# Float64 weights to float32: one VectorE shift-and-or in place of a VectorE shift and a GpSimd integer sum, and all weight remainders on VectorE

## The chip, the core and the metric

One core of a Trainium2 chip runs the whole program. Its engines are TensorE (PE; PEld is its weight load), VectorE (DVE), ScalarE (ACT), GpSimd (POOL) and SyncE (SP), whose queue issues the transfers here. The metric is the device time of one execution in microseconds (us), lower is better.

## The reference

Four batches of an attention with a linear memory beside it, then two feed-forward blocks over the 2304 tokens:

```python
a = softmax(causal(q @ k.T / 8)); local = a @ v               # B=4, H=8, S=576, D=64
mem = (phi(q) @ M_prev) / (phi(q) . z_prev + 1e-6)
x = sigmoid(beta) * mem + (1 - sigmoid(beta)) * local          # tokens x 512
x = ((x @ w1) * (x @ w2)) @ w3 @ w_out                         # 512 -> 1024 -> 512
out = (sigmoid(x @ w_gate) * (x @ w_val)) @ moe2_w_out         # 512 -> 1536 -> 512
```

The feed-forward weights arrive as float64, 8 bytes a number. The kernel has to make float32 of them on the chip.

## The kernel before, in words

**Work and stages.** The batches run one after another, and batch b's feed-forward part (`ffn`) is woven with batch b+1's attention (`attention`). In the profile the feed-forward products carry the names of what they make: `wps` (a product of w3 and w_out, made once, by `prep`), `ab` (x with w1 and w2), `xw` (times that product), `gv` (gate and value), `ot` (the output). Each weight is used as a float32r head plus a float32r remainder, so a product takes three matmuls. PE's order is written out by hand; the other engines' orders come from a scheduler that goes by priority, and that follows the order in which the program emits its steps.

**The weights' way.** All 76 float64 pieces (128 x 512 numbers, 512 KB each) are converted in batch 0, inside the first 370 us. A piece goes like this:

- SP loads it to `r` (line 279; three buffers).
- `conv_step`, step 0: ACT makes `cy` from the high words (L307) and `cr` from the low words (L308). `cy` are the bits of the float32 result, shifted right by three places; `cr` is the low word's top three bits, rounded to an integer from 0 to 8. Two buffers each. The next load is emitted here, too.
- step 1: DVE shifts `cy` left by three into `wraw` (L316; three buffers of two pieces each).
- step 2: POOL adds `cr` to `wraw` as integers (L320). A second piece of a unit that is needed again whole is then written to DRAM as `kf` (L322).
- `split_step` calls `split_rows`: ACT copies `wraw` to a float32r head (L549), and DVE or POOL takes the remainder (L551), into `wslot` (a ring of five) or, for w_out, `wo`. `SHARE_W` says which engine: 0.2 of the pieces on POOL in the start, 0.5 in batch 0's feed-forward. What later batches read again is written to DRAM as `k` (L419).

`pump`, called after every second group of matmuls, emits at most one `conv_step` and one `split_step`; `prep` emits one or the other per yield while the first four `wo` pieces are missing.

**What else is on these engines around there.** POOL scales the attention's probabilities `p` (L870) and takes two products of the memory path, `me` and `mphi` (L782, L791). DVE takes the score reductions (L844), the products `hraw` and `hgraw` (L623, L688), and the remainders of activations, `h` and `hg` (L551 too). ACT takes the exponentials (L116), the sigmoid of the gate, `gsb` (L116), and copies out of PSUM. After the conversion the `wraw` buffers hold `wagain`, weights read back from `kf`, of which `make_step` makes sums (`wmade`) for later batches.

Of the kernel before, what the change touches and what calls it, by code (L numbers as in the profile page):

```python
# [10 lines left out]
U32 = mybir.dt.uint32  # L11
# [3 lines left out]
AF = mybir.ActivationFunctionType  # L15
ALU = mybir.AluOpType
# [19 lines left out]
P0 = 8  # L36
NPREP = 4

SHARE_W = (0.2, 0.5, 0.0, 0.0)
SHARE_H = (0.0, 0.0, 0.3, 0.4)  # L40
SHARE_X = (0.0, 0.4, 0.5, 0.5)
SHARE_N = (1.0, 0.5, 0.5, 0.5)
# [5 lines left out]
EXPO = 0x7F800000  # L48
TOP = 2.0**13
MOST = 2.0**45  # L50

FRAC = 0.96
FA = (1.0, 1.0)
# [6 lines left out]
def tile_attention_memory_ffn(  # L60
# [17 lines left out]
    nc = tc.nc  # L78
# [58 lines left out]
    def power(out, back, sums):  # L137
# [4 lines left out]
        nc.vector.tensor_scalar(a, sums.bitcast(I32), EXPO, EXPO, ALU.bitwise_and, ALU.bitwise_xor)  # L142
        nc.vector.tensor_scalar(out, a.bitcast(F32), TOP, MOST, ALU.mult, ALU.min)
        nc.vector.tensor_scalar(b, out.bitcast(I32), EXPO, EXPO, ALU.bitwise_and, ALU.bitwise_xor)
# [80 lines left out]
    ws = {"conv": 0, "step": 0, "split": 0, "ring": 0, "freed": 0, "use": 0, "again": 0, "mstep": 0, "pumps": 0, "late": 0, "scaled": 0, "wo": 0, "pass": 0, "wready": False}  # L225
    tmp = {}
# [47 lines left out]
    def load64(n):  # L274
        if n < len(conv_slots):
            s = conv_slots[n]
            t = fp.tile([128, 512], I64, tag="r64", name=f"r64_{s}", bufs=R64)
            src = units[s // 2][0][s % 2]
            d = nc.sync.dma_start(out=t, in_=src.rearrange("p a c -> p (a c)"))
            raw64[s] = t  # L280
            last["dma"] = d

    def whole(u, hf):
        return raws[u][:, 4 * hf : 4 * hf + 4, :].rearrange("p a c -> p (a c)").bitcast(I32)

    def conv_step():
        s = ws["conv"]
        u, hf = divmod(s, 2)
        if u >= NU or (ws["step"] == 0 and ws["split"] < 2 * (u - 2)):
            return False  # L290
        src = units[u][0]
        if not isinstance(src, list):
            if not ws["wready"]:
                return False
            raws[u] = fp.tile([128, 8, 128], F32, tag="wraw", name=f"wraw{u}", bufs=3)
            last["dma"] = nc.sync.dma_start(out=raws[u], in_=src)
            ws["conv"] += 2
            return True
        if ws["step"] == 0:
            w = raw64.pop(s).bitcast(I32).rearrange("p (c two) -> p c two", two=2)  # L300
            y = fp.tile([128, 512], F32, tag="cy", name=f"cy{s}", bufs=2)
            r = fp.tile([128, 512], I32, tag="cr", name=f"cr{s}", bufs=2)
            hi = w[:, :, 1].bitcast(F32)

            nc.scalar.activation(out=y, in_=hi, func=AF.Prelu, scale=2.0**-112, alpha=2.0**32)  # L307
            nc.scalar.activation(out=r, in_=w[:, :, 0].bitcast(U32), func=AF.Copy, scale=2.0**-29)  # L308
            load64(conv_rank[s] + R64)
            tmp["y"], tmp["r"] = y.bitcast(I32), r  # L310
            ws["step"] = 1
        elif ws["step"] == 1:
            if hf == 0:
                raws[u] = fp.tile([128, 8, 128], F32, tag="wraw", name=f"wraw{u}", bufs=3)
            y, z = tmp["y"], whole(u, hf)
            nc.vector.tensor_scalar(z, y, 3, None, ALU.logical_shift_left)  # L316
            ws["step"] = 2
        else:
            z = whole(u, hf)
            nc.gpsimd.tensor_tensor(z, z, tmp["r"], ALU.add)  # L320
            if hf == 1 and u in kept:
                nc.sync.dma_start(out=kept[u], in_=raws[u])  # L322
            ws["step"] = 0
            ws["conv"] += 1
        return True
# [12 lines left out]
    def make_step():  # L338
# [21 lines left out]
        src = src[:, 0::3] if m == 0 else src[:, 1:3]  # L360
        split_rows(t.rearrange("p x (a b) c -> p x a (b c)", b=2), src, SHARE_W)
        nc.sync.dma_start(out=summed[makes[k]][m], in_=t.bitcast(F32))
# [32 lines left out]
    def split_step():  # L395
# [7 lines left out]
        if not units[u][1]:  # L403
# [4 lines left out]
            wot[m] = t  # L408
            split_rows(t[:, :, :DM].rearrange("p x (a c) -> p x a c", c=128), r, SHARE_W)
            ws["wo"] += 1  # L410
        else:
# [3 lines left out]
            w = fp.tile([128, 2, 4, 128], F32R, tag="wslot", name=f"wslot{n}", bufs=RING)  # L415
            split_rows(w, r, SHARE_W)
            if s in stored:
# [8 lines left out]
    def pump():  # L426
        late_scale()
        late_load()
        conv_step()
        split_step()  # L430
        ws["pumps"] += 1
        if phase["n"] == 2 and ws["pumps"] % 2 == 0:
            make_step()

    def need(store, s):
        while s not in store:
            moved = split_step()
            moved = conv_step() or moved
            ws["pumps"] += 1
            late_scale()  # L440
            late_load()
            assert moved
        return store[s]
# [104 lines left out]
    def split_rows(dst, src, share=None):  # L548
        nc.scalar.copy(dst[:, 0], src)  # L549
        eng = lower(share) if share else nc.vector  # L550
        eng.tensor_sub(dst[:, 1], src, dst[:, 0].bitcast(F32))  # L551

    def prep(g):
        p, f0 = divmod(2 * g, F1)
        for m in range(4 * p, 4 * p + 4):
            while m not in wot:
                if not split_step():
                    conv_step()
                yield WAIT
# [622 lines left out]
```

## Time and profile before

| what | before |
|---|---|
| median of 3 runs | 1068.26 us (1065.63 to 1071.70) |
| the profiled execution's own time | 1070.48 us |
| its span (first to last instruction) | 1068.70 us |
| PE busy | 1029.2 us, 96% |
| DVE busy | 610.9 us, 57% |
| ACT busy | 559.5 us, 52% |
| POOL busy | 401.7 us, 38% |

Busy times are sums over the span, so an average over stages that have different limits. PE's busy time includes the tail of matmuls whose ends are modelled, so a stage with PE at 96% may still have room. The stages in the profile's time: the start (attention of batch 0 and the first half of `wps`) up to 129 us, `ab` to 240, `xw` to 272, `gv` to 352, `ot` to 402, and then batch 1. The clock of PE is full in most slices; it reads 0.87 and 0.74 of full in 40 to 80 us.

### The profile page before, as it was taken

The numbers are of one execution on the slowest core, as the hardware profiler recorded it, in microseconds if no ns is written. First come the engines' busy times: TensorE is split into PE (matmuls) and PEld (weight loads), VectorE is DVE, ScalarE is ACT, GpSimd is POOL, SyncE is SP. The second block draws the span as 40 slices with busy tenths as digits, with TensorE's granted clock in tenths as the row PEclk, the third lists the DMA queues.
The fourth block names the chain that finished last, engine by engine and source line by source line (L and its number), as shares of the span: only waits on it lengthen the run. The fifth ranks groups of instructions, "written<-read, shape, count | busy, mean of one in ns | idle before, by whom it ended". The sixth has DMA issues, their size and how long they took to land.

```text
span 1068.7 us, 20275 instructions
## 1 busy us (share of the span) xinstructions
PE 1029.2 (96%) x7408; PEld 892.7 (84%) x7408; DVE 610.9 (57%) x1457; ACT 559.5 (52%) x1195; POOL 401.7 (38%) x352
## 2 busy tenths in 40 slices
PE   7899999999999998999999998999999999999998
PEld 3455687888999898898998886777999898899998
DVE  6765678756567657995755438754666321226630
ACT  6877687657767735564533444564544332224420
POOL 5967576436567702332233102322334200003320
PEclk9889999999999999999999998999999999999999
DMA  8664799958999589994688646522599543248981
GB/s 264 199 204 135 245 331 342 330 178 301 302 348 333 181 309 407 337 333 142 226 305 292 195 146 232 177 73 73 177 331 324 187 139 132 82 155 308 324 286 54
DMA packets 92667, 252.13 MB, mean 236 GB/s; under 512 B 11544, under 2 KB 30104, under 8 KB 92568
## 3 DMA queue, kind: packets, MB, share of 16 engines
q1 hardware_dynamic: 92568, 250.84, 68.4%
q8 instruction: 59, 0.97, 0.4%
q14 instruction: 40, 0.33, 0.1%
HBM read 186.31 MB, written 64.49 MB: 235 GB/s over the span
## 4 chain that ended last, share of the span: by engine, by line
PE 66%; DMA 6%; DVE 4%; issue 2%; ACT 2%; POOL 2%; SPq 1%; DVEq 0%; POOLq 0%; ACTq 0%
PE gvp L476 16%; PE ab L465 16%; PE ot L465 10%; PE xw L465 9%; PE gv L465 5%; PE s L839 3%; PE t L900 3%; PE o L968 2%; DMA wagain<-kf 2%; DMA wslot<-s 2%; PE o L953 1%; DMA k<-wslot 1%; PE o L961 1%; DMA wraw<-kf 1%; POOL wraw L320 1%
## 5 line engine op out<-in xcount | busy, mean ns | idle before, releaser
L465 PE MATMUL ab<-x,wslot 128*128 128x288 f32 (+1 forms) x1536 | 221.4, 297 | 0.4 <-DMA wslot<-k 0.4
L476 PE MATMUL gvp<-x,wslot 128*128 128x288 f32 x1512 | 204.5, 296 | 4.8 <-DMA wslot<-s 3.1
L476 PEld LDWEIGHTS gvp<-x,wslot 128*128 128x128 f32 x1512 | 202.0, 188 | 7.0 <-DVE hgraw L545 4.8
L870 POOL TENSOR_SCALAR p<-p,sm,omg 116x116 f32<-116x116 f32 (+4 forms) x100 | 88.3, 886 | 220.3 <-DVE sm L868 151.3
L465 PE MATMUL ot<-hg,wslot 128*128 128x288 f32 x1152 | 163.7, 298 | 1.3 <-DVE hg L551 1.3
L465 PEld LDWEIGHTS ot<-hg,wslot 128*128 128x128 f32 x1152 | 154.4, 188 | 7.4 <-issue 5.1
L116 ACT ACTIVATE p<-p,sm 116x116 f32<-116x116 f32 (+4 forms) x160 | 93.2, 583 | 68.8 <-DVE sm L844 65.8
L320 POOL TENSOR_TENSOR wraw<-wraw,cr 128x512 int32<-128x512 int32 x76 | 110.1, 1463 | 29.0 <-DVE wraw L316 26.8
L465 PE MATMUL xw<-h,wslot 128*128 128x288 f32 x768 | 111.9, 299 | 1.2 <-DVE h L551 0.9
L465 PEld LDWEIGHTS ab<-x,wslot 128*128 128x128 f32 x768 | 105.5, 190 | 8.1 <-issue 5.6
L465 PEld LDWEIGHTS xw<-h,wslot 128*128 128x128 f32 x768 | 103.3, 188 | 4.9 <-issue 2.4
L844 DVE CUSTOM_DVE_ANT_0 p<-s,msk 116x116 f32<-116x116 f32 (+4 forms) x160 | 68.3, 453 | 63.3 <-PE s L839 62.7
L465 PEld LDWEIGHTS <-wslot 128*128 128x128 f16 x768 | 74.0, 99 | 22.1 <-issue 3.1
L900 PE MATMUL t<-idf,p 116*116 116x116 f32 x480 | 70.5, 275 | 11.6 <-DVE sm L867 4.7
L465 PE MATMUL gv<-x,wslot 128*128 128x288 f32 x576 | 78.3, 296 | 2.0 <-DVE hgraw L688 1.4
L465 PEld LDWEIGHTS gv<-x,wslot 128*128 128x128 f32 x576 | 76.6, 188 | 3.6 <-DVE hgraw L688 2.5
L900 PEld LDWEIGHTS t<-idf,p 116*116 116x116 f32 x480 | 54.7, 140 | 27.6 <-ACT p L116 7.2
L526 POOL TENSOR_TENSOR u4gv<-u2gv,s5gv 128x288 f32<-128x288 f32 x36 | 29.3, 813 | 116.4 <-ACT s5gv L524 74.0
L551 POOL TENSOR_TENSOR wslot<-wraw,wslot 128x512 fp32r<-128x512 f32 x36 | 47.8, 1327 | 52.6 <-ACT wslot L549 49.0
L623 DVE TENSOR_TENSOR hraw<-ab,asb 128x288 f32<-128x288 f32 x64 | 29.1, 454 | 62.8 <-PE ab L465 60.3
L307 ACT ACTIVATE cy<-r 128x512 f32<-128x512 f32 x76 | 50.4, 672 | 24.1 <-DVE wraw L316 12.0
L308 ACT ACTIVATE cr<-r 128x512 int32<-128x512 uint32 x76 | 50.9, 671 | 12.1 <-POOL wraw L320 11.4
(127 smaller groups left out, 1547.0 us busy)
## 6 DMA issues: line engine op xcount, KB each, us to landing
wslot<-k SPq DMA_DIRECT2D x112, 512.0 KB, 4.7
wslot<-s SPq DMA_DIRECT2D x72, 512.0 KB, 4.9
k<-wslot SPq DMA_DIRECT2D x48, 512.0 KB, 4.7
r<-in_gv_dram SPq DMA_DIRECT2D x24, 512.0 KB, 5.4
s<-wmade SPq DMA_DIRECT2D x24, 512.0 KB, 5.6
kf<-wraw SPq DMA_DIRECT2D x20, 512.0 KB, 5.3
qk<-in_qk_dram SPq DMA_DIRECT2D x32, 290.0 KB, 4.3
wslot<-k SPq DMA_DIRECT2D x36, 256.0 KB, 4.6
```

What stands on the lines that cost most here:

```text
L116: ins = nc.scalar.activation(**kw)
L307: nc.scalar.activation(out=y, in_=hi, func=AF.Prelu, scale=2.0**-112, alpha=2.0**32)
L308: nc.scalar.activation(out=r, in_=w[:, :, 0].bitcast(U32), func=AF.Copy, scale=2.0**-29)
L320: nc.gpsimd.tensor_tensor(z, z, tmp["r"], ALU.add)
L465: nc.tensor.matmul(ps, w[:, wi, blk, :], x[:, xi, cols : cols + n], start=first and part == 0, stop=last and part == 2,)
L476: nc.tensor.matmul(ps, w[:, wi, blk + k, :], x[:, xi, k, :], start=k == 0 and part == 0, stop=k == 1 and part == 2,)
L526: nc.gpsimd.tensor_add(u4, u2, s5)
L551: eng.tensor_sub(dst[:, 1], src, dst[:, 0].bitcast(F32))
L839: nc.tensor.matmul(os_[hh], q_[r, 0, i * T : (i + 1) * T], k_[r, 1, c0:c1], start=x == 0, stop=x == len(terms) - 1,)
L844: nc.vector.tensor_tensor_reduce(out=ps_[hh][:, c0:c1], in0=os_[hh], in1=msk[:, SP - w + c0 : SP - w + c1], scale=-0.125, scalar=3.0e38 if ...
L870: lower(SHARE_N).tensor_scalar(ps_[hh][:, :w], ps_[hh][:, :w], sm[:, 6 + hh : 7 + hh], omg[:T, 2 * p + hh : 2 * p + hh + 1], ALU.mult, ALU ...
L900: nc.tensor.transpose(tp[:T, c : c + T], src[hh][:, j * T : (j + 1) * T], idf[:T, :T])
```

## The change

Step 2 goes away. The low word's top three bits are now scaled by 7/8 of the former factor and get a bias just under 0.5, so that `cr` is an integer from 0 to 7, which fits in the three bits that the shift leaves free. DVE shifts `cy` and sets these bits in one instruction with two inputs. `SHARE_W` becomes zero in all phases, so that every weight remainder is DVE's. A conversion is now two calls of `conv_step` instead of three.

```diff
-SHARE_W = (0.2, 0.5, 0.0, 0.0)
+SHARE_W = (0.0, 0.0, 0.0, 0.0)
+HALF = 0.5 - 2.0**-12
+LAST3 = 2.0**-29 * 7 / 8
...
-            nc.scalar.activation(out=r, in_=w[:, :, 0].bitcast(U32), func=AF.Copy, scale=2.0**-29)
+            nc.scalar.activation(out=r, in_=w[:, :, 0].bitcast(U32), func=AF.Copy, scale=LAST3, bias=HALF)
...
-            nc.vector.tensor_scalar(z, y, 3, None, ALU.logical_shift_left)
-            ws["step"] = 2
-        else:
-            z = whole(u, hf)
-            nc.gpsimd.tensor_tensor(z, z, tmp["r"], ALU.add)
+            nc.vector.scalar_tensor_tensor(z, y, 3, tmp["r"], ALU.logical_shift_left, ALU.bitwise_or)
             if hf == 1 and u in kept:
                 nc.sync.dma_start(out=kept[u], in_=raws[u])
             ws["step"] = 0
```

Line numbers move with it: L307, L308, L316, L549, L551 and L870 are L310, L311, L319, L548, L550 and L869 in the changed kernel. The instruction streams of all engines come out in another order. POOL has 114 rows less (76 sums, 38 remainders), DVE 38 more.

POOL's queue at the start of the program, before (`p`: probabilities of the attention, `me` and `mphi`: its memory path, `wraw`: weights):

```order
L870 TENSOR_SCALAR p_0_0_1_243<-p_0_0_1_243,sm_0_0_244,omg 116x116
L320 TENSOR_TENSOR wraw_273<-wraw_273,cr_233 128x512
L782 TENSOR_TENSOR me_0_251<-mphi_0_252,z_0_218 116x640
L870 TENSOR_SCALAR p_0_1_0_264<-p_0_1_0_264,sm_0_1_266,omg 116x232
L870 TENSOR_SCALAR p_0_1_1_265<-p_0_1_1_265,sm_0_1_266,omg 116x232
L870 TENSOR_SCALAR p_0_2_0_285<-p_0_2_0_285,sm_0_2_287,omg 116x348
L870 TENSOR_SCALAR p_0_2_1_286<-p_0_2_1_286,sm_0_2_287,omg 116x348
L320 TENSOR_TENSOR wraw_273<-wraw_273,cr_309 128x512
L791 TENSOR_TENSOR mphi_0_252<-mphi_0_252,mn_0_253 116x640
```

and now:

```order
L869 TENSOR_SCALAR p_0_0_1_243<-p_0_0_1_243,sm_0_0_244,omg 116x116
L781 TENSOR_TENSOR me_0_251<-mphi_0_252,z_0_218 116x640
L869 TENSOR_SCALAR p_0_1_0_264<-p_0_1_0_264,sm_0_1_266,omg 116x232
L869 TENSOR_SCALAR p_0_1_1_265<-p_0_1_1_265,sm_0_1_266,omg 116x232
L869 TENSOR_SCALAR p_0_2_0_287<-p_0_2_0_287,sm_0_2_289,omg 116x348
L869 TENSOR_SCALAR p_0_2_1_288<-p_0_2_1_288,sm_0_2_289,omg 116x348
L790 TENSOR_TENSOR mphi_0_252<-mphi_0_252,mn_0_253 116x640
```

The weights' sums no longer stand between the attention's instructions; the attention's own order on POOL is the same.

ACT's queue around one unit of the `gv` stage (unit 5; `gsb`: the sigmoid of one half of the gate, `cy` and `cr`: the conversion of two pieces that come later, `wslot` and `hg`: heads), before:

```order
L116 ACTIVATE gsb_5_0_3734<-gv_5_0_0_3714 128x288
L307 ACTIVATE cy_3791<-r_68_3659 128x512
L308 ACTIVATE cr_3792<-r_68_3659 128x512
L307 ACTIVATE cy_3831<-r_69_3707 128x512
L308 ACTIVATE cr_3832<-r_69_3707 128x512
L116 ACTIVATE gsb_5_1_3772<-gv_5_1_0_3757 128x288
L549 CAST wslot_3781<-wraw_3545 128x512
L549 CAST wslot_3811<-wraw_3633 128x512
L549 CAST hg_5_3712<-hgraw_5_3713 128x576
```

and now:

```order
L119 ACTIVATE gsb_5_0_3681<-gv_5_0_0_3656 128x288
L310 ACTIVATE cy_3731<-r_68_3593 128x512
L311 ACTIVATE cr_3732<-r_68_3593 128x512
L310 ACTIVATE cy_3761<-r_69_3649 128x512
L119 ACTIVATE gsb_5_1_3712<-gv_5_1_0_3699 128x288
L548 CAST wslot_3721<-wraw_3491 128x512
L311 ACTIVATE cr_3762<-r_69_3649 128x512
L548 CAST wslot_3751<-wraw_3577 128x512
L548 CAST hg_5_3654<-hgraw_5_3655 128x576
```

The second sigmoid of the unit stands ahead of the second `cr` now. The units differ: in some both `cr` still stand ahead of it.

DVE's queue around the same unit (`hgraw`: the product of gate and value), before:

```order
L551 TENSOR_TENSOR wslot_3723<-wraw_3545,wslot_3723 128x512
L316 TENSOR_SCALAR wraw_3721<-cy_3703 128x512
L551 TENSOR_TENSOR hg_4_3624<-hgraw_4_3625,hg_4_3624 128x576
L316 TENSOR_SCALAR wraw_3721<-cy_3743 128x512
L688 TENSOR_TENSOR hgraw_5_3713<-gv_5_0_1_3736,gsb_5_0_3734 128x288
L688 TENSOR_TENSOR hgraw_5_3713<-gv_5_1_1_3774,gsb_5_1_3772 128x288
```

and now:

```order
L319 SCALAR_TENSOR_TENSOR wraw_3663<-cy_3645,cr_3646 128x512
L319 SCALAR_TENSOR_TENSOR wraw_3663<-cy_3675,cr_3676 128x512
L550 TENSOR_TENSOR wslot_3665<-wraw_3491,wslot_3665 128x512
L550 TENSOR_TENSOR hg_4_3568<-hgraw_4_3569,hg_4_3568 128x576
L687 TENSOR_TENSOR hgraw_5_3655<-gv_5_0_1_3683,gsb_5_0_3681 128x288
L550 TENSOR_TENSOR wslot_3721<-wraw_3491,wslot_3721 128x512
L687 TENSOR_TENSOR hgraw_5_3655<-gv_5_1_1_3714,gsb_5_1_3712 128x288
```

Both remainders of a unit are on DVE now, one of them between the two products.

## Rows read from the trace of the kernel before

**Rows 1.** The page, part 1: busy us (share of the span) xinstructions.

```profile
PE 1029.2 (96%) x7408; PEld 892.7 (84%) x7408; DVE 610.9 (57%) x1457; ACT 559.5 (52%) x1195; POOL 401.7 (38%) x352
```

**Rows 2.** Windows by stage: length, busy us of PE, PEld, DVE, ACT, POOL; PEclk, DMA, GB/s.

```profile
8.00:62.00 54.00, 48.05 (x178) 24.27 (x178) 44.32 (x103) 44.80 (x102) 44.98 (x41) 0.94 0.77 242
62.00:129.00 67.00, 66.16 (x329) 41.47 (x330) 39.27 (x110) 46.15 (x110) 41.36 (x42) 0.92 0.57 182
129.00:240.00 111.00, 105.20 (x731) 88.42 (x729) 79.44 (x182) 77.28 (x166) 62.23 (x48) 0.98 0.84 290
272.00:352.00 80.00, 78.00 (x576) 76.38 (x576) 53.66 (x71) 57.41 (x108) 51.70 (x36) 1.00 0.96 335
402.00:460.00 58.00, 53.94 (x411) 46.86 (x410) 49.96 (x135) 32.77 (x80) 17.24 (x13) 1.00 0.98 368
```

**Rows 3.** The same windows of line L320 alone (POOL).

```profile
8.00:62.00 54.00, 21.39 (x16) 0.94 0.77 242
```

**Rows 4.** The same windows of line L551 alone (DVE, POOL).

```profile
8.00:62.00 54.00, 8.48 (x9) 2.57 (x2) 0.94 0.77 242
```

**Rows 5.** Windows of 20 us, all engines, as in rows 2.

```profile
20.00:40.00 20.00, 17.29 (x62) 8.06 (x61) 16.68 (x44) 18.33 (x45) 18.80 (x18) 0.96 0.70 212
120.00:140.00 20.00, 17.43 (x100) 13.33 (x96) 18.48 (x34) 13.60 (x29) 15.18 (x12) 0.91 0.78 241
```

**Rows 6.** The chain that ended last, 302 to 309 us: start, us, what.

```profile
302.24 0.43 DVE wraw L316
...
302.74 1.74 POOL wraw L320
...
304.85 1.29 POOL wraw L320
...
306.16 0.02 ACT cr L308
...
306.73 0.41 ACT gsb L116
...
307.18 1.86 PE gv L465 x12
```

**Rows 7.** The same chain at its end: output products with nothing beside them.

```profile
1026.94 38.17 PE ot L465 x288
```

**Rows 8.** The same chain at 235 and at 372 us.

```profile
235.62 1.71 DVE wslot L551
...
372.54 1.29 POOL wslot L551
...
374.23 5.10 DMA wagain<-kf
```

**Rows 9.** Groups by line and form: count | busy us, mean ns | idle before.

```profile
L320 POOL TENSOR_TENSOR wraw<-wraw,cr 128x512 int32<-128x512 int32 x76 | 110.1, 1463 | 29.0 <-DVE wraw L316 26.8 <-ACT cr L308 1.9 <-DVE mn L787 0.4
L551 POOL TENSOR_TENSOR wslot<-wraw,wslot 128x512 fp32r<-128x512 f32 x36 | 47.8, 1327 | 52.6 <-ACT wslot L549 49.0 <-DMA k<-wslot 3.5
L551 DVE TENSOR_TENSOR wslot<-wraw,wslot 128x512 fp32r<-128x512 f32 x40 | 45.8, 1146 | 16.0 <-ACT wslot L549 15.6
```

**Rows 10.** Single lines and tiles: duration ns min/median/max, first and last start us.

```profile
L316 DVE TENSOR_SCALAR wraw<-cy x76: 368/421/1522, 8.8 to 365.8; 128x512 int32<-128x512 int32 x76
L551 DVE TENSOR_TENSOR wslot<-wraw,wslot x40: 672/1003/1823, 38.3 to 384.5; 128x512 fp32r<-128x512 f32 x40
L780 DVE SCALAR_TENSOR_TENSOR mphi<-qnr,me x16: 803/818/1739, 11.9 to 753.9; 116x640 f32<-116x640 f32 x16
L308 ACT ACTIVATE cr<-r x76: 647/672/704, 8.7 to 361.0; 128x512 int32<-128x512 uint32 x76
```

**Rows 11.** The windows of rows 2 of line L316 alone (DVE).

```profile
8.00:62.00 54.00, 12.82 (x16) 0.94 0.77 242
129.00:240.00 111.00, 9.31 (x18) 0.98 0.84 290
272.00:352.00 80.00, 17.18 (x24) 1.00 0.96 335
```

## The prediction

> **What bounds the kernel now.** I read the page's busy shares first, then the windows by stage, then the chain of waits, and last the durations of single lines. PE is busy for 96% of the span [rows 1], so at most some 40 us of 1068.7 can be had by filling its gaps, and the change touches only the first 370 us: no conversion runs later. The windows [rows 2] say which stages have room. From 8 to 62 us, four engines share the load: POOL 45.0 us of 54, ACT 44.8, DVE 44.3, PE 48.1, and PE's clock is at 0.94 of full. From 62 to 129 us PE is busy for 66.2 of 67 us. From 129 to 240 us it idles 111 - 105.2 = 5.8 us, in `gv` 2.0 us, from 402 to 460 us 4.1 us, in the last two with the DMA engines at 0.96 and 0.98.
>
> Idle time alone hides what slow feeding costs in `gv`. Output products with nothing beside them run 288 in 38.17 us [rows 7], 0.1325 us each. The 576 of `gv` would need 76.3 us and take 80.0. Where the 3.7 us go, the chain shows [rows 6]: a shift on DVE, a POOL sum of 1.74 us, a second of 1.29 us, then ACT's `cr`, which waited for the buffer that the sum gave back, then the sigmoid `gsb` behind it in ACT's queue, and only then PE. So a sum on POOL holds up a sigmoid, through ACT's order, and that holds up PE.
>
> **The price of the new instructions.** No row shows a shift with an or of two tensors on DVE. The nearest are DVE instructions with two tensors in SBUF. A `scalar_tensor_tensor` of 116 x 640 has a median of 818 ns [rows 10]; by columns that is 818 x 512/640 = 654 ns for 512. The remainder of 128 x 512 takes 672 ns at its shortest, with a median of 1003 [rows 10] and a mean of 1146 [rows 9]. The ends are thus 0.65 and 1.15 us. The long ones fall where POOL works on weights at the same time, and that work goes away; I take 0.68, next to the shortest. The shift that is removed has a median of 421 ns, but a mean of 0.68 us over the 58 of the three stages below: (12.82 + 9.31 + 17.18)/58 [rows 11].
>
> So DVE gets, per piece, 0.68 for about 0.68, and 38 remainders of 0.68 that POOL had, 26 us. POOL loses 110.1 us of sums [rows 9] and 38 x 1.33 = 50 us of remainders, 160 of its 402. ACT's `cr` gets a bias beside its scale: I cost that at nothing, since the line takes 672 ns with a scale alone [rows 10] and its element count is the same. The transfers are the same in number and size; SP's queue gets them in a slightly other order. Each conversion being two calls instead of three, pieces are emitted earlier, but the rings (three `r`, five `wslot`) limit how far ahead they get.
>
> **Term A, 8 to 62 us.** POOL loses 21.4 us [rows 3] and 2.6 us [rows 4] of its 45.0, and is left with 21.0 in 54. The attention's scaling of `p` then no longer stands behind sums, and DVE's short steps no longer beside them. ACT is late next: its 44.8 us stay. In its fullest stretch, 20 to 40 us, it is busy for 18.33 of 20 [rows 5]; at that pace 44.8 us of work take 48.9. The gain is 54 - 48.9 = **5.1 us**. Ends: nothing, if the chain through ACT and DVE is as long as before; 9.2, if ACT never waits. DVE allows it: 44.3 - 12.8 + 18 x 0.68 = 43.7 us of 48.9.
>
> What the row of the shift shows here is 368 ns at the shortest and 1522 at the longest; the 1.15 us between them are about the length of a POOL instruction (1.29) [rows 6]. The Trainium skill ("SBUF — State Buffer", section "SBUF: two separate sides") calls the port pair that the two engines share an exclusive lock: a DVE instruction with two SBUF inputs also waits for a POOL instruction that reads SBUF, to its end. By that rule the new instructions keep some waiting, since POOL still has 21.0 us of attention work in this stage. An estimate by it: a chance of 21/54 to meet one, about half a POOL instruction of 1.3 us lost each time, so 0.25 us on each of 18, 4.5 us of DVE; at the highest pace that DVE shows, 18.48 of 20 [rows 5], its 48.2 us take 52.2 and term A is 1.8 instead of 5.1.
>
> **Term B, 129 to 240 us.** PE's 5.8 us of idle are the upper end, nothing the lower. At 235.6 us the chain runs through a DVE remainder of 1.71 us [rows 8], 1.0 above the shortest; that ends. Of the other 4.8 I give a quarter to POOL's weight work. **2 us.**
>
> **Term C, `gv`.** The two sums leave the chain (1.74 + 1.29 us, where a unit takes 80/12 = 6.7 us on average), a fused instruction and a bit of DVE's queue come in. DVE has the time: 53.7 - 17.2 [rows 11] + 36 x 0.68 = 61 of 80 us, even if nothing else gets shorter. Then PE's own 76.3 us bind, or the transfers, which are at 0.96 of the 16 engines already. Ends 0 and 3.7. I take two thirds, **2.5 us**.
>
> **Term D, 352 to 460 us.** Before batch 1, `wagain` waits for a buffer that a POOL remainder of 1.29 us frees [rows 8]; on DVE it is 0.6 shorter, and the last pieces come a little earlier. From 402 us the transfers bind (0.98), and PE idles 4.1 us, the upper end. **1 us.**
>
> The sum is 5.1 + 2 + 2.5 + 1 = 10.6 us. The profiled execution took 1070.48 us (span 1068.70), so 1059.9; it stands 2.2 us above the median of the runs, 1068.26, from which the same sum gives **1058 us**. With every term at its upper end, 22.8 us, it would be 1045.5.
>
> **The rivals.**
> 1. *Nothing is left of it.* The waits on POOL go, and the same stages are held by what stands next: in `gv` and after 402 us the transfers (0.96 and 0.98), from 8 to 62 us DVE. With A at 1.8, B at 1, C and D at nothing, the gain is 2.8 us: 1065.5. For it: both DMA shares. Against it: batch 1 moves 368 GB/s while `gv` moves 335 [rows 2], so the engines can do a tenth more. The Trainium skill warns of the same outcome for a move between these two engines ("Perfetto Trace Analysis", section "Optimizing Scalar/DVE Operations"): they share a port, so it might not help. The rows bear that out for the two-input work on DVE only while POOL is at work, and in `gv` POOL has nothing left.
> 2. *DVE becomes the engine that binds, and the kernel is slower.* The place is the fused instructions and remainders on DVE in the three stages; the price is the contended 1.146 us each instead of 0.68. DVE then needs 44.3 - 12.8 + 18 x 1.146 = 52.1 of 54 us; from 129 to 240 us 79.4 - 9.3 + (18 + 12) x 1.146 = 104.5 of 111; in `gv` 53.7 - 17.2 + 36 x 1.146 = 77.8 of 80. At its highest pace, 18.48 of 20, these take 56.4, 113.1 and 84.2 us: 8.7 us longer together, 1077. It begins to decide from about 1.05 us a piece. Against it: the long remainders lie beside POOL's weight work, of which none is left.
> 3. *More than the terms.* PE fills up early, so that its clock, 0.92 of full from 62 to 129 us, holds (0.08 x 67 = 5.4 us), and three of the four terms come near their ends: some 20 us, 1048.
>
> That the change does not do what it says is small here: POOL's rows are gone from its queue. What may miss is that the new order of all engines costs or gives a few us by itself; that lies in the ranges.
>
> **How the numbers follow.** Forecast 0.54 (its own range 1050 to 1063), nothing 0.28, more 0.07, slower 0.11. The range of 8 in 10 runs from 1047, which takes in the third rival, to 1068, which takes in the first; the second is left out. About 0.5%, 5.3 us, is what a measurement here can tell from no change, so faster means under 1062.9 and slower above 1073.6. Faster: 0.53 of the forecast, 0.01 of the first rival, 0.07 of the third, 0.61. Same: 0.01 + 0.27 + 0.02 of the second, 0.30. Slower: 0.09.
>
> **What would show it.** In the profile after, the fused line should have 76 instructions with a median near 0.68 us, and the remainders of `wslot` on DVE a mean well under 1.0; a mean over 1.05 of either is rival 2. POOL should fall from 402 to about 240 us. `gv` should last 76.5 to 78 us; if it stays at 80 with the DMA share near 0.96, term C is wrong and rival 1 right there. The first `ab` matmul, at 129 us now, should come 4 to 6 us earlier; earlier than 120 us would be rival 3. If ACT in the first 62 us is no fuller than 0.83, it was not ACT that stood next, and term A's reason is wrong whatever its size.

## The result, and the profile after

| | before | changed |
|---|---|---|
| median | 1069.19 us (1065.63 to 1071.70, 6 runs) | 1056.65 us (1051.99 to 1060.08, 6 runs) |
| the profiled execution's span | 1068.7 us | 1055.7 us |
| mean granted clock of PE | 0.987 | 0.992 |

The ratio is 0.9885, 95% interval 0.9854 to 0.9917: faster by 12.5 us. The prediction said 1058.0.

Page of the changed kernel, part 1 [rows 1]:

```profile
PE 1024.9 (97%) x7408; PEld 892.2 (85%) x7408; DVE 592.8 (56%) x1495; ACT 557.4 (53%) x1195; POOL 240.6 (23%) x238
```

The windows by stage and of 20 us, columns as in [rows 2, 5]. The stages now start earlier, so the same window holds some of the next one: the window from 272 to 352 us holds 16 us of `ot`. The fifth line is `gv` in its own time.

```profile
8.00:62.00 54.00, 53.89 (x213) 28.96 (x214) 41.30 (x123) 49.93 (x119) 24.64 (x26) 1.00 0.79 261
62.00:129.00 67.00, 63.74 (x334) 41.02 (x333) 40.74 (x119) 48.14 (x113) 23.54 (x28) 0.92 0.62 209
129.00:240.00 111.00, 110.41 (x799) 95.03 (x798) 78.01 (x196) 78.74 (x170) 21.91 (x19) 1.00 0.87 305
272.00:352.00 80.00, 78.00 (x588) 76.31 (x587) 52.85 (x98) 58.94 (x112) 2.94 (x2) 1.00 0.84 302
...
258.80:335.90 77.10, 76.54 (x578) 76.31 (x577) 46.78 (x82) 57.96 (x110) 0.00 (x0) 1.00 0.97 342
...
20.00:40.00 20.00, 20.00 (x63) 10.29 (x61) 12.79 (x38) 19.07 (x45) 6.69 (x6) 1.00 0.79 246
40.00:60.00 20.00, 20.00 (x110) 11.70 (x109) 15.50 (x47) 18.40 (x46) 7.81 (x10) 1.00 0.71 236
...
120.00:140.00 20.00, 18.37 (x116) 14.80 (x114) 14.75 (x37) 16.49 (x37) 2.18 (x3) 1.00 0.97 355
```

One such window of the kernel before, which [rows 5] do not have:

```profile
40.00:60.00 20.00, 18.91 (x93) 12.13 (x93) 15.96 (x30) 16.04 (x33) 17.32 (x15) 0.87 0.69 209
```

From 8 to 62 us PE went from 48.05 to 53.89 us, POOL from 44.98 to 24.64, ACT from 44.80 to 49.93. The clock no longer falls from 20 to 60 us (0.96 and 0.87 before, 1.00 now). From 120 to 140 us it reads 1.00 instead of 0.91, but not in a second profile of the same kernel, which the experiments brought:

```profile
120.00:140.00 20.00, 18.21 (x108) 15.43 (x107) 13.43 (x32) 16.52 (x37) 2.17 (x3) 0.91 0.97 350
```

The products by name show where the stages start: after the durations (ns, shortest, median, longest) stand the first and the last start. Kernel before:

```profile
L465 PE MATMUL ab<-x,wslot x1536: 282/290/589, 129.0 to 933.5; 128*128 128x288 f32 x96, 128*128 128x288 f16 x96
L465 PE MATMUL gv<-x,wslot x576: 288/294/400, 272.2 to 352.3; 128*128 128x288 f32 x192
```

Changed kernel:

```profile
L464 PE MATMUL ab<-x,wslot x1536: 283/290/448, 121.6 to 920.5; 128*128 128x288 f32 x96, 128*128 128x288 f16 x96
L464 PE MATMUL gv<-x,wslot x576: 288/294/398, 258.8 to 335.8; 128*128 128x288 f32 x192
```

Read so for every stage (the last column is that second profile):

| first product, us | before | changed | changed, again |
|---|---|---|---|
| `ab`, batch 0 | 129.0 | 121.6 | 121.9 |
| `xw` | 234.2 | 221.7 | 223.3 |
| `gv` | 272.2 | 258.8 | 260.5 |
| `ot` | 352.4 | 335.9 | 337.6 |
| `ab`, batch 1 | 402.7 | 387.0 | 388.7 |
| `gvp` (gate and value), batch 1 | 520.6 | 505.1 | 506.8 |
| `ot`, batch 1 | 594.1 | 580.8 | 577.7 |
| end of the span | 1068.7 | 1055.7 | 1052.4 |

The start gains 7.4 us, `ab` 5.1, `xw` 0.9, `gv` 3.1; then 0.8 are given back in `ot`, and in this execution 2.2 more in batch 1's `gvp`, which the second profile does not repeat.

What became of the pieces: the groups of the new instruction, of the remainders and of the two ACT instructions that open a conversion. Behind the second bar stands how long the engine idled just before them, and for whom. Before, for ACT (for DVE it is [rows 9]):

```profile
L308 ACT ACTIVATE cr<-r 128x512 int32<-128x512 uint32 x76 | 50.9, 671 | 12.1 <-POOL wraw L320 11.4
L307 ACT ACTIVATE cy<-r 128x512 f32<-128x512 f32 x76 | 50.4, 672 | 24.1 <-DVE wraw L316 12.0 <-ACT gsb L116 3.8 <-issue 2.8
```

After:

```profile
L550 DVE TENSOR_TENSOR wslot<-wraw,wslot 128x512 fp32r<-128x512 f32 x76 | 54.5, 719 | 34.1 <-ACT wslot L548 31.8 <-DMA k<-wslot 2.1
L319 DVE SCALAR_TENSOR_TENSOR wraw<-cy,cr 128x512 int32<-128x512 int32 x76 | 53.7, 732 | 1.6 <-ACT cr L311 1.1
L310 ACT ACTIVATE cy<-r 128x512 f32<-128x512 f32 x76 | 51.5, 677 | 9.2 <-DVE wraw L319 2.0 <-issue 1.6 <-DMA r<-in_w3t_dram 1.6
L311 ACT ACTIVATE cr<-r 128x512 int32<-128x512 uint32 x76 | 50.8, 669 | 0.0
```

The durations of the new line, as in [rows 10]:

```profile
L319 DVE SCALAR_TENSOR_TENSOR wraw<-cy,cr x76: 629/684/1920, 8.6 to 348.5; 128x512 int32<-128x512 int32 x76
```

ACT waited 36.2 us ahead of the conversions, mostly for DVE and POOL to give `cy` and `cr` back; now it waits 9.2. This wait is the one to follow through the experiments, because the sigmoids and the copies that PE needs stand behind it in ACT's queue.

### The profile page after: what moved, and what is told of

It reads as the page before. It is cut to its first block, busy times and chain, and to the rows that moved or that the text cites. A ratio compares the mean times of both kernels' runs of the same rounds, so it can differ in the third digit from the quotient of the medians.

```text
span 1055.7 us, 20138 instructions
## 1 busy us (share of the span) xinstructions
PE 1024.9 (97%) x7408; PEld 892.2 (85%) x7408; DVE 592.8 (56%) x1495; ACT 557.4 (53%) x1195; POOL 240.6 (23%) x238
## 4 chain that ended last, share of the span: by engine, by line
PE 83%; DMA 6%; DVE 5%; ACT 3%; issue 1%; POOL 1%; SPq 0%; ACTq 0%; DVEq 0%; POOLq 0%
PE ab L464 17%; PE gvp L475 16%; PE ot L464 12%; PE xw L464 8%; PE gv L464 7%; PE s L838 6%; PE t L899 5%; PE wps L464 4%; PE o L967 4%; DMA wslot<-s 2%; PE o L952 2%; DMA wraw<-kf 1%; PE o L960 1%; DMA r<-in_gv_dram 1%; DVE p L843 1%
## 5 line engine op out<-in xcount | busy, mean ns | idle before, releaser
L869 POOL TENSOR_SCALAR p<-p,sm,omg 116x116 f32<-116x116 f32 (+4 forms) x100 | 86.4, 869 | 336.5 <-DVE sm L867 247.3
L550 DVE TENSOR_TENSOR wslot<-wraw,wslot 128x512 fp32r<-128x512 f32 x76 | 54.5, 719 | 34.1 <-ACT wslot L548 31.8
L310 ACT ACTIVATE cy<-r 128x512 f32<-128x512 f32 x76 | 51.5, 677 | 9.2 <-DVE wraw L319 2.0
L548 ACT CAST wslot<-wraw 128x512 fp32r<-128x512 f32 x76 | 47.2, 622 | 14.5 <-PE gv L464 4.2
L464 PE MATMUL wps<-wo,wslot 128*128 128x512 f32 x192 | 54.8, 422 | 0.0
```

Source lines behind the costliest of these rows:

```text
L464: nc.tensor.matmul(ps, w[:, wi, blk, :], x[:, xi, cols : cols + n], start=first and part == 0, stop=last and part == 2,)
L869: lower(SHARE_N).tensor_scalar(ps_[hh][:, :w], ps_[hh][:, :w], sm[:, 6 + hh : 7 + hh], omg[:T, 2 * p + hh : 2 * p + hh + 1], ALU.mult, ALU ...
```

## The experiments

The runs came in three groups, each with the kernel before beside it (median 1067.66, 1068.28 and 1067.60 us); each ratio is to the kernel before of the same group.

### The two parts apart

The fused instruction alone is the changed kernel with

```diff
-SHARE_W = (0.0, 0.0, 0.0, 0.0)
+SHARE_W = (0.2, 0.5, 0.0, 0.0)
```

> The changed kernel with its fused instruction, but with the old shares of the remainders: 0.2 of them on POOL in the start, 0.5 in batch 0's feed-forward. Theory 1 (the gain of 12.5 us comes from POOL's sums leaving the weights' chain and POOL's queue): most of it stays, 8 to 12 us, so 1057 to 1061 us, and the first ab matmul comes at 121 to 123 us as in the changed kernel, since only 2 remainders were on POOL before 62 us. Theory 2 (the remainders' move makes the gain): at most 3 us are left, 1066 to 1069, and the first ab matmul stays near 129. If both parts are needed together, it lies between, 1061 to 1066.

The remainders alone are the kernel before with

```diff
-SHARE_W = (0.2, 0.5, 0.0, 0.0)
+SHARE_W = (0.0, 0.0, 0.0, 0.0)
```

> The kernel before with all weight remainders on DVE, and the shift and POOL's sum kept. Theory 1 (the sums): 0 to 4 us are gained, 1065 to 1069 us, the first ab matmul stays within 2 us of 129, and the remainders on DVE keep a mean near 1.1 us beside POOL's sums, so that it may even lose a little. Theory 2 (the remainders): 8 us or more, under 1061. If the two parts add up, the gains of this run and of the one with the fused instruction alone give 12.5 us together.

Measured: 1050.79 us, 0.9841 (0.9816 to 0.9867), and 1071.11 us, 1.0031 (1.0007 to 1.0055). The fused instruction makes the whole gain, and more than was expected (16.9 us); the remainders' move by itself loses 3.4 us. In the second run POOL's sums take 1544 ns on average (1463 before) and ACT's waits ahead of the conversions stay, at 31.5 us:

```profile
L308 ACT ACTIVATE cr<-r 128x512 int32<-128x512 uint32 x76 | 51.1, 675 | 14.4 <-POOL wraw L320 14.3
L307 ACT ACTIVATE cy<-r 128x512 f32<-128x512 f32 x76 | 50.5, 676 | 17.1 <-DVE wraw L316 4.8 <-DMA r<-in_gv_dram 3.0 <-issue 2.7
```

Parts of the expectations missed. With the fused instruction alone the first `ab` came at 125.5, not at 121 to 123: seven remainders were on POOL ahead of it, of which only two start before 62 us. With the remainders alone the time lies above the 1065 to 1069 us expected, and the first `ab` came at 126.2. In its profile `ab` takes 109.3 us (105.2 before) and `ot` 54.2 (50.3 before), while the start and `gv` are shorter.

### Is it the shorter emission?

```diff
             nc.vector.scalar_tensor_tensor(z, y, 3, tmp["r"], ALU.logical_shift_left, ALU.bitwise_or)
+            ws["step"] = 2
+        else:
```

> The changed kernel with an empty third call in each conversion, so that its pieces are emitted at the pace of the kernel before. Theory 1 (the sums on POOL): no difference of over 3 us, 1054 to 1060 us. Theory 4 (the gain comes from the shorter emission, by which pieces stand earlier in the scheduler's order): 5 us or more of the gain go, 1062 us or later, with the first ab matmul after 125 us.

Measured: 1054.43 us, 0.9867 (0.9836 to 0.9898), the first `ab` at 120.3. Emission in two calls rather than three is no part of the gain that a measurement here can tell.

### POOL's sums back, beside the weights' way

A sum with a column of zeros on the piece in `wraw`, after its remainder, so that no head and no remainder needs it:

```diff
+        if isinstance(units[u][0], list):
+            nc.gpsimd.tensor_tensor(whole(u, hf), whole(u, hf), zero.to_broadcast([128, 512]), ALU.add)
```

> The changed kernel with 76 integer sums of 128x512 given back to POOL, each adding a column of zeros to a wraw piece after its remainder was taken, so that no weight waits for them except through the reuse of the buffer. POOL's busy time goes back to about 350 us. Theory 1 in its narrow form (what counts is that a weight no longer waits for POOL): the time stays within 3 us of the changed kernel, 1054 to 1060 us. Theory 3 (what counts is that POOL's work no longer stands beside DVE's two-input instructions, and before the attention's scaling in POOL's queue): most of the gain goes, 1063 to 1069 us, and the mean of the fused instructions and of the remainders rises from 0.73 to over 1.0 us.

Measured: 1070.42 us, 1.0012 (0.9993 to 1.0032). All of the gain goes, though nobody needs the sums. The mean of the fused instructions rose to 0.92 us and that of the remainders to 0.79, less than the 1.0 of the third theory. The two theories of the expectation are not told apart by that alone: the sum stands beside DVE's instructions, and it is also the last to touch the buffer that the next unit waits for. The next run keeps the first and drops the second, and it has no sums in the start before 110 us.

```diff
+        if isinstance(units[u][0], list) and phase["n"] == 1 and ("t" in side or not pending):
...
+                z = side["t"].bitcast(I32)
+                tc.add_manual_dep(
+                    nc.gpsimd.tensor_tensor(z, z, zero[: z.shape[0]].to_broadcast([z.shape[0], 512]), ALU.add).ins,
+                    last["rem"].ins.name,
...
```

> As the run with POOL sums set aside, but each sum now adds zeros to a tile that nothing else uses at that time (116 or 128 x 512, started when the piece's remainder is done), so that no weight buffer waits for it, and only after the start: some 60 sums from 130 to 370 us. Theory 3a (POOL's sums stretch the DVE instructions beside them): the ab stage takes 103 us or more and gv 81 us or more, as in that run (104.8 and 82.7), the fused instructions and remainders get a mean of 0.8 us or more, and the time is 1063 us or later. Theory 3b (there it was the wraw buffer that the sum held back): ab and gv take 100 and 77 us as in the changed kernel, and the time is 1052 to 1059 us.

Measured: 1059.14 us, 0.9915 (0.9895 to 0.9935), with 63 sums. The groups of the run that held the buffer:

```profile
L423 POOL TENSOR_TENSOR wraw<-wraw,zero 128x512 int32<-128x512 int32 x76 | 92.9, 1226 | 122.9 <-DVE wslot L554 106.0 <-DVE wo L554 4.4 <-POOL wraw L423 4.1
L321 DVE SCALAR_TENSOR_TENSOR wraw<-cy,cr 128x512 int32<-128x512 int32 x76 | 68.0, 921 | 3.3 <-POOL wraw L423 2.3 <-ACT cr L313 1.0
L312 ACT ACTIVATE cy<-r 128x512 f32<-128x512 f32 x76 | 51.3, 676 | 37.3 <-issue 26.1 <-DVE wraw L321 4.6 <-DMA r<-in_w_dram 1.4
```

and of the run on the idle tile:

```profile
L430 POOL TENSOR_TENSOR side<-side,zero 116x512 int32<-116x512 int32 x34 | 40.9, 1203 | 78.1 <-DVE wslot L565 76.0 <-PE s L859 2.1
L322 DVE SCALAR_TENSOR_TENSOR wraw<-cy,cr 128x512 int32<-128x512 int32 x76 | 72.0, 973 | 1.3 <-ACT cr L314 1.1
L313 ACT ACTIVATE cy<-r 128x512 f32<-128x512 f32 x76 | 51.4, 676 | 18.4 <-DVE wraw L322 4.7 <-issue 2.4 <-ACT hg L563 2.3
```

The fused instructions are longer in the second (973 ns against 921 and 732), and yet `gv` runs there from 260.6 to 337.5, 76.9 us, as in the changed kernel (77.0); with the buffer held it takes 82.6. Both runs have 24 sums in that stage. `ab` takes 102.4 us on the idle tile (23 sums) and 104.8 with the buffer held (19 sums); the changed kernel's two profiles have 100.1 and 101.4. So of the 10 us lost in these two stages by the held buffer, the stretching of DVE's instructions explains at most 2, and the buffer, with the order that follows from it, some 8: the stretching of theory 3a came, but the stage times are those of 3b. Another 3.3 us were lost ahead of the first `ab` (124.9 against 121.6), where the idle tile had 6 sums and the held buffer 21; there the two are not told apart. The timeline (start, us, engine, line, idle before) shows how, with the buffer held:

```profile
275.39 1.38 DVE L554 TENSOR_TENSOR wslot<-wraw,wslot 128x512 fp32r<-128x512 f32 x1
...
276.70 0.75 DVE L554 TENSOR_TENSOR hg<-hgraw,hg 128x576 fp32r<-128x576 f32 x1
276.91 1.43 POOL L423 TENSOR_TENSOR wraw<-wraw,zero 128x512 int32<-128x512 int32 x1 [0.68 <-POOL wraw L423]
277.37 2.13 DVE L321 SCALAR_TENSOR_TENSOR wraw<-cy,cr 128x512 int32<-128x512 int32 x2
278.97 0.68 ACT L312 ACTIVATE cy<-r 128x512 f32<-128x512 f32 x1 [2.48 <-issue]
...
281.21 0.40 ACT L121 ACTIVATE gsb<-gv 128x288 f32<-128x288 f32 x1
```

and on the idle tile:

```profile
293.31 0.45 DVE L702 TENSOR_TENSOR hgraw<-gv,gsb 128x288 f32<-128x288 f32 x1
293.54 1.04 POOL L430 TENSOR_TENSOR side<-side,zero 116x512 int32<-116x512 int32 x1 [1.76 <-DVE wslot L565]
293.68 2.05 DVE L322 SCALAR_TENSOR_TENSOR wraw<-cy,cr 128x512 int32<-128x512 int32 x2
...
295.24 0.67 ACT L313 ACTIVATE cy<-r 128x512 f32<-128x512 f32 x1
...
295.65 0.68 DVE L565 TENSOR_TENSOR wslot<-wraw,wslot 128x512 fp32r<-128x512 f32 x1
```

A pair of fused instructions takes 2.1 us in both. On the idle tile it stands right behind the product `hgraw`, ahead of the next remainder, and `cy` follows with no idle time. With the buffer held it stands behind the second remainder and the remainder of `hg`; ACT idles 2.48 us before `cy` (the profile names no releaser, but `cy` starts while the pair runs, and the pair frees its buffer), and the sigmoid `gsb` comes after it. This order is shown; that the scheduler chose it because the pair must wait for POOL's sums is the likely reason and not shown. DVE itself hardly waits for POOL there (2.3 us in the whole run).

### More on DVE

One instruction more per piece, a maximum over the piece, which nobody waits for (its result is not used):

```diff
+            nc.vector.tensor_reduce(fp.tile([128, 4], F32, tag="aside", name=f"aside{s}", bufs=1), z.bitcast(F32).rearrange("p (a c) -> p a c", a=4), AX.X, ALU.max)
```

> The changed kernel with one more DVE instruction per piece, a maximum over the 128x512 result that nobody reads, some 0.65 us each, 49 us more of DVE in the first 370 us, and no more work on POOL. If DVE's own time bounds the weights' stages (the second rival of the prediction, which decides from about 1.05 us a piece), 0.65 more on 0.73 is far beyond that point: 1070 us or later. If DVE has the room that its busy shares show (41 of 54 us, 78 of 111, 53 of 80), it costs under 4 us: 1053 to 1060 us.

and the shift and the or as two instructions:

```diff
-            nc.vector.scalar_tensor_tensor(z, y, 3, tmp["r"], ALU.logical_shift_left, ALU.bitwise_or)
+            nc.vector.tensor_scalar(z, y, 3, None, ALU.logical_shift_left)
+            nc.vector.tensor_tensor(z, z, tmp["r"], ALU.bitwise_or)
```

> The changed kernel with the shift and the or as two DVE instructions, 0.42 and about 0.68 us: nothing on POOL, 76 instructions more on DVE, 28 to 32 us. Theory 1 and 3 (the gain is POOL's absence, not the single instruction): within 3 us of the changed kernel, 1053 to 1060 us. If the fusion itself counts, that is the shorter way of a piece on DVE: 1062 us or later.

Measured: 1060.32 us, 0.9927 (0.9900 to 0.9954), and 1062.11 us, 0.9935 (0.9912 to 0.9959). The first adds 51.4 us of DVE and lands 3.9 us above the changed kernel's later measurement (1056.42, below), just over the range expected. By stages it costs nothing in the start (first `ab` at 120.8) and nothing in `gv` (77.1 us), but `ab` takes 106.6 us: there DVE does bind. The second adds 33.1 + 50.9 - 53.7 = 30.3 us and costs no less, 5.7 us. Its first `ab` comes at 124.4, so most of the start's gain is there without POOL; but `ab` takes 105.1 us and `gv` 79.9, as before the change. In `ab` both lose in the same place, between 122 and 131 us, where PE waits once for a probability (total, times, longest; the changed kernel's second profile, then the maximum, then the two instructions):

```profile
PE t L899 <- DVE p L869: 1.8, 1, 1.8
...
PE t L900 <- DVE sm L868: 6.0, 1, 6.0
...
PE t L900 <- DVE p L870: 3.9, 1, 3.9
```

From 120 to 140 us the clock then reads 0.74 and 0.83. The run with the remainders alone has a wait of the same kind, of 4.1 us. So the loss in `ab` goes with the length of DVE's queue ahead of the attention's steps, whether a weight needs the instruction or not. In the start and in `gv` it is the way of the piece that counts: there the maximum costs nothing, and the two instructions cost 2.8 and 2.9 us. Their row of `cr` has the wait that the fused instruction does not have:

```profile
L311 ACT ACTIVATE cr<-r 128x512 int32<-128x512 uint32 x76 | 50.1, 672 | 6.2 <-DVE wraw L320 6.1
```

The intervals of these two and of the changed kernel touch, so each difference by itself is not told apart from none with certainty; the stages, PE's waits and the row of `cr`, of one profile each, carry the reading.

### What is next in the start, and the place of the remainders

```diff
-SHARE_T = (0.1, 0.0, 0.0, 0.0)
+SHARE_T = (0.35, 0.0, 0.0, 0.0)
```

> The changed kernel with a third of the start's copies of transposed probabilities out of PSUM on DVE in place of ACT (0.35 instead of 0.1). If ACT is what stands next in the start, as the prediction says (it is busy for 49.9 of 54 us from 8 to 62 us), the first ab matmul comes 2 to 4 us before 121.6 and the time is 1050 to 1054 us. If PE itself is now the limit there (53.9 of 54 us), nothing changes before 62 us and the time stays at 1054 to 1060 us; it is slower if DVE's chain gets longer by it.

Measured: 1052.17 us, 0.9854 (0.9824 to 0.9883), the first `ab` at 115.5. The start ends 6.1 us earlier, more than expected, but not where it was expected: from 8 to 62 us PE does 219 matmuls instead of 213, and the clock reads 0.91 from 40 to 60 us, where the changed kernel has 1.00. The difference lies behind, first in the changed kernel, then here:

```profile
60.00:80.00 20.00, 18.37 (x75) 10.40 (x72) 10.41 (x40) 13.64 (x36) 10.59 (x14) 0.74 0.58 185
```

```profile
40.00:60.00 20.00, 18.90 (x95) 11.84 (x95) 15.23 (x50) 18.19 (x44) 10.96 (x13) 0.91 0.76 247
60.00:80.00 20.00, 19.88 (x108) 12.28 (x109) 16.08 (x52) 16.13 (x43) 13.87 (x18) 1.00 0.72 228
```

From 60 to 80 us PE idles 0.12 us here instead of 1.63, and the clock stays full. By the medians, taking work from ACT helps, by 4 to 5 us here and in the table below, though with intervals that overlap; what it gives comes with the clock, and the two are not told apart. Then, side by side, with `SHARE_W = (0.0, 0.5, 0.0, 0.0)`, the same with the new `SHARE_T`, and the changed kernel again:

> The changed kernel with half of the remainders of batch 0's feed-forward on POOL again, nothing else. If the move of the remainders to DVE cost something (DVE then has a shorter queue ahead of the next piece), 1049 to 1053 us, with a gain over the changed kernel run beside it of 2 to 6 us. If the remainders' place makes no difference, it stays within 2 us of the changed kernel.

> The changed kernel with half of the remainders of batch 0's feed-forward on POOL again, as before, and 0.35 of the start's copies of transposed probabilities on DVE. If the two add up (the fused instruction with the old shares gave a time 3.6 us under the changed kernel with the third call, and the copies 4 us under the changed kernel in its first measurement, in other calls of the chip), it comes to 1046 to 1050 us, the first ab matmul at 115 to 117 us. If they gain the same microseconds, or if the transfers bind, 1050 to 1054 us.

> The changed kernel once more, so that the others stand beside it on one chip: 1053 to 1058 us, ratio 0.986 to 0.990, and in the profile gvp of batch 1 longer than 73.5 us if its wait for the transfers is the kernel's and not one execution's.

| | median, us | ratio (interval) |
|---|---|---|
| half of the remainders of batch 0's feed-forward on POOL | 1052.76 | 0.9860 (0.9822 to 0.9898) |
| that, and the copies on DVE | 1047.51 | 0.9808 (0.9778 to 0.9839) |
| the changed kernel again | 1056.42 | 0.9888 (0.9861 to 0.9916) |

Both edits together beat the changed kernel by 8.9 us, with intervals that don't meet; it has the lowest median of all here. Its first `ab`, at 113.5, came earlier than the 115 to 117 expected. The remainders' place alone is 3.7 us with overlapping intervals: likely, not settled. The last run also settles the give-back in batch 1. PE's waits (total, times, longest) from 470 to 600 us in the first profile of the changed kernel:

```profile
PE gvp L475 <- DMA wslot<-s: 4.8, 5, 1.3
```

and in the second:

```profile
PE gvp L475 <- DMA wslot<-s: 1.6, 2, 1.2
```

The same program waited 3.2 us more for the same loads in one execution than in the other, and `gvp` took 75.7 and 70.9 us (73.5 before). That is scatter between executions and not the change's: of the 4.8 us these waits are 3.2, and the rest is not traced. The expectation of over 73.5 us missed.

## Why the prediction was right, and where it was not

- **The sum.** 10.6 us were forecast, 12.5 measured, inside the forecast's own range. The mechanism held, but the closeness is in part luck: A, B and C measured 15.6 us together in the first profile where 9.6 were forecast, D came with the wrong sign, and `gvp` gave back 2.2 us by scatter.
- **Price of the fused instruction.** Taken as 0.68 us, median 0.684, mean 0.732. Right, as is that the bias in `cr` costs nothing (671 ns before, 669 after). The remainders' mean fell from 1146 to 719 ns. POOL came to 240.6 us, as said.
- **Term A, 5.1 us; measured 7.4 and 7.1.** POOL's queue was freed, and ACT is as full as forecast (49.93 of 54 us, 0.925, forecast 0.917). That ACT set the pace is not shown: PE itself reads 53.89 of 54, and the copies on DVE gave PE only 6 matmuls more by 62 us. The step that failed is the size: the term let ACT's pace set the stage and gave the clock no part. It read 0.96 and 0.87 of full from 20 to 60 us, a mixture of 1.2 and 2.4 GHz, while PE idled 2.7 and 1.1 us of each 20; with PE busy for 20.00 of 20 it reads 1.00. On full windows 0.17 x 20 = 3.4 us of PE's time came back there, an estimate from these rows. That the idle time made the clock fall is not shown: from 120 to 140 us the changed kernel idles 1.63 us at 1.00 in one profile and 1.79 us at 0.91 in the other. The third rival looked for the clock's gain only from 62 to 129 us, where it stayed at 0.92.
- **The lock.** In the start the fused instructions average 11.42/16 = 0.714 us by the windows of their line. The 0.25 us that the prediction added, following the Trainium skill ("SBUF — State Buffer", section "SBUF: two separate sides"), did not come, nor did the 1.8 us for term A that followed from it. Beside sums that always fall on them they do stretch: from 258 to 337 us on the idle tile, 24.25 us for 24, 1.01 each. So the trace agrees with the rule that such an instruction waits for POOL's; the guess at how often it strikes in the start was too high, and in `gv` the stretch cost nothing.
- **Term B, 2 us; measured 5.1 and 3.8.** The size failed: of 4.8 us of PE's idle time the term gave a quarter to POOL's weight work, as a guess, and the 5.8 us from 129 to 240 us fell to 0.6. The term named a DVE remainder at 235 us; the experiments point to the stage's beginning, where DVE was busy for 18.48 of 20 us [rows 5] and is now for 14.75 and 13.43. With the maximum, with two instructions or with the remainders moved alone PE waits there for DVE, and the stage takes 105 to 109 us. The clock is no steady part of it: from 120 to 140 us it reads 1.00 in the one profile and 0.91, as before, in the other.
- **Term C, 2.5 us; measured 3.1 in both.** Right in size and place: 77.0 us against a floor of 76.3. The share of the DMA engines in the stage's own time is 0.97 (258.8 to 335.9 us), no lower than before (0.96). So a share this high did not mean that the transfers bind, which the first rival took it for.
- **Term D, 1 us; measured -1.0.** Wrong in sign: `ot` and batch 1's `ab` and `xw` together take 1.0 us longer (168.2 to 169.2). The buffer comes back sooner (the first load of `wagain` is issued 20.2 us after the first `ot`, 21.8 before), but at the place of [rows 8] the chain of the changed kernel runs through two transfers (start, us, what):

```profile
376.09 6.75 DMA wslot<-k
...
382.91 8.64 DMA s<-wmade
```

- **Rivals.** Nothing left: did not come. The Trainium skill ("Perfetto Trace Analysis", section "Optimizing Scalar/DVE Operations") warns that a move between these two engines may not help; the move of the remainders alone agrees (1.0031). The fused instruction gained (0.9841); it is more than a move, since the shift was DVE's already. DVE binds: did not come in the changed kernel. Its point of decision, 1.05 us a piece, was too low for the whole kernel: 735 + 676 ns a piece still beat the kernel before by 0.7%. In `ab` it had the right place, since the maximum took the stage's whole gain there. For work on the piece's way it was nearer: 465 + 690 ns gave back half of the gain.
- **What the prediction did not weigh.** It treated both parts of the change as help. The remainders' move alone loses 3.4 us; in its profile `ab` and `ot` are the longer stages.

Not tried: the start's own split between the clock and ACT, and sums on an idle tile before 110 us.

## What to carry to other kernels

Of a chain of small steps over few buffers, count who gives each buffer back, and in which place of its engine's queue: an instruction that nobody needs cost the whole gain here, some 8 of 14 us because it was the last to touch the buffer. A stretched instruction is not yet a loss (1.01 for 0.68 us cost nothing in `gv`), and whether a busy engine binds changes by the stage (the maximum on DVE cost 5 to 6 us in `ab` and nothing in `gv`); the idle time ahead of the steps that feed PE shows both. Where a profile has a clock under full beside PE idle time, a change may give back the clock too, as from 20 to 60 us here: price it apart, and look at a second profile before counting on it.

## What the runs showed of the hardware

- A shift-and-or of two 128x512 int32 tiles on DVE takes 684 ns, the or alone 684 and the shift alone 419 (medians): in the fused form the shift costs nothing.
- Beside a POOL sum of 1.2 us that falls on it, that shift-and-or takes 1.01 us on average.
- Two executions of one program differed by 4.8 us in one stage of 71 to 76 us, 3.2 of it in their waits for the same loads, and by 1.00 and 0.91 in the clock from 120 to 140 us.
